# K and Q loaded at a unit's first step over two queues, row maxima 21 steps ahead, the first output weights loaded at the chunk's end

## The chip, the cores and the metric

The kernel runs on one core of one Trainium2 chip. The metric is the device time of one execution in microseconds (us), lower is better, as the median of several runs. Names used below: PE is the engine for matmuls, DVE the vector engine, ACT the scalar engine, POOL the GpSimd engine, SP the engine that only issues DMAs. The core has 16 DMA engines. DMAs are put to them through queues: q1 in the profile is filled by SP, q0 by POOL.

## The reference

One transformer block with conditioned layer norms, softmax attention with 32 heads of width 16, and a SwiGLU feed-forward part, for 2048 tokens of width 512, in float32:

```python
def _A_ref(x, wqkv, wo):
    B, S, D = x.shape
    H = 32; Dh = D // H
    qkv = (lambda x, *d: x.transpose(*d))((x @ wqkv).reshape(B, S, 3, H, Dh), 2, 0, 3, 1, 4)
    q, k, v = qkv[0], qkv[1], qkv[2]
    scale = Dh ** -0.5
    scores = jnp.einsum("bhqd,bhkd->bhqk", q, k) * scale
    p = _softmax(scores, axis=-1)
    o = jnp.einsum("bhqk,bhkd->bhqd", p, v)
    return (lambda x, *d: x.transpose(*d))(o, 0, 2, 1, 3).reshape(B, S, D) @ wo

def _B_ref(x, w_gate, w_up, w_down):
    g = _silu(x @ w_gate)
    u = x @ w_up
    return (g * u) @ w_down

mod = (_silu(c) @ w_mod).reshape(c.shape[0], 6, 1, -1)
sa, ca, ga, sb, cb, gb = (mod[:, 0], mod[:, 1], mod[:, 2], mod[:, 3], mod[:, 4], mod[:, 5])
h = _layernorm(x, axis=-1) * (1 + ca) + sa
x = x + ga * _A_ref(h, A_wqkv, A_wo)
h = _layernorm(x, axis=-1) * (1 + cb) + sb
x = x + gb * _B_ref(h, B_w_gate, B_w_up, B_w_down)
```

S is 2048, D is 512, F (the width of the feed-forward part) is 1792.

## The kernel before

**Stages.** The start (to about 190 us) computes Q, K and V. Each float32 operand is split in a high and a low half (`split`, L201), and a product is three matmuls (`mm3`, L205). Q and K are written to the DRAM tensors qd and kd, V stays on the chip in v_flat. The ten blocks of the weights wqs that are still to be split then are made by `weights` (L337): ACT writes the high half (L202) and the engine given to `split_w` the low half (L203), which is DVE for the blocks of K (j == 1) and POOL for the others. The bank of a projection is emptied by ACT (L367) and DVE (L369) into prt.

**Units and steps.** Attention runs over 32 units: unit u is a group of 4 heads (NG = 8 groups) and one of 4 chunks of 512 query tokens, with eight units to a chunk. A unit has 16 steps, one for each 128 keys. A step has four score matmuls (`score`, L506, each followed by an exp on ACT), four matmuls with their row maxima (`max_one`, L479 on PE and L481 on DVE) and the products with V (`pv_step`, L521). The maxima run `LEAD` = 20 steps ahead of the scores, so they belong to the next unit but one or the next. The first LEAD - 1 steps of maxima stand in a loop at the end of the start stage, between the last projection matmuls (`take(late, 9)`, nine matmuls to a step). When a unit's maxima are complete, `max_rows` (L483) reduces them on DVE, transposes them on PE (L491 to L493), and SP writes them as two further rows into the Q tile (L497, `qop<-mr`). The first score of that unit waits for this.

**Loads of a unit.** K of a unit goes into one of three kop tiles, Q into one of three qop tiles (`load_k`, `load_q`, `load_parts` at L401). The rows lie in two halves: partitions 0 to 47 and 64 to 111, one DMA for each half, 768 KB for K and 192 KB for Q. The function `before` puts the loads for unit u + 2 into the program ahead of step 6 of unit u. The tiles they write were last read by the scores of unit u - 1.

**The end of a unit** (`close_unit`, L836) comes two steps into the next: the denominators are copied out of the result o (`out_a`, `dn<-o`, L532), inverted on DVE (L536, two steps later), written to DRAM (L537, `d_dr<-dn`) and read back spread over all rows (L542, `rb<-d_dr`). All these DMAs are SP's. POOL multiplies (L548) and stores (L549). After the last unit of a chunk come the chunk's output weights wo (`load_wo`, L643): four steps after the close for chunk 0, one for the others.

**Filling.** From units 9, 17 and 25 on the steps of a chunk's successors are mixed with the output projection and the FFN of the finished chunk (`filled`, L944; the weights wgu and wd are loaded by SP, L652 and L657). A step without such work is called plain here, one with it filled. In units 1 to 7, POOL splits the FFN weights (`split_weights`, L575) and stores them to DRAM.

**What sets the order.** The kernel is written in the order of issue: each engine executes its instructions in the order of the program, and a wait of one holds everything behind it on the same engine. That holds for SP and POOL as issuers of DMAs too. An engine that has nothing to wait for runs ahead of the others.

Of the kernel before, what the change touches and what calls it, by code (L numbers as in the profile page):

```python
# [9 lines left out]
F32 = mybir.dt.float32  # L10
# [9 lines left out]
P = 128  # L20
S = 2048
D = 512
# [4 lines left out]
NK = D // P  # L27
NC = 4
CW = S // NC
NG = H // 4  # L30
NU = NG * NC
# [3 lines left out]
SCALE = DH ** -0.5  # L35
HD = D // 2
HQ = CW // 2
LEAD = 20
KR = 48
WIN = 3  # L40
HALVES = (2, 1, 1, 2)
# [1 line left out]
UG = 16 * NG  # L43
# [11 lines left out]
def run(it):  # L55
    for _ in it:
        pass


def take(it, k):  # L60
    run(islice(it, k))
# [40 lines left out]
def block_kernel(ctx, tc, x, wqkv, wo, w_gate, w_up, w_down, c, w_mod, out):  # L102
    nc = tc.nc
# [28 lines left out]
    qd = dram.tile([D, 3, S], F32, name="qd")  # L132
    kd = dram.tile([D, 3, S], F32, name="kd")
# [67 lines left out]
    def split(dst_h, dst_l, src, eng):  # L201
        nc.scalar.copy(dst_h, src)  # L202
        eng.tensor_sub(dst_l, src, dst_h.bitcast(F32))  # L203
# [11 lines left out]
    kop = [vp.tile([P, 2, S], F32R, name="kop0"), None, None]  # L215
# [20 lines left out]
    def stage(name):  # L236
        return pa.tile([P, NK, D], F32, name=name, tag="wst", bufs=3)
# [6 lines left out]
    def load_x(ci):  # L244
        xt[ci] = new_x()
        nc.sync.dma_start(xt[ci], xd[:, 4 * ci:4 * ci + 4, :])
# [6 lines left out]
    for ab in range(2):  # L253
        wm_ab.append(stage(f"wm_ab{ab}"))
        for e, v in enumerate((1, 0)):
            c0 = v * D + ab * HD
# [43 lines left out]
    def split_w(src, c0, eng=nc.gpsimd):  # L300
        cols = slice(c0, c0 + P)
        split(wqs[0][:, :, cols], wqs[1][:, :, cols], src, eng)
# [34 lines left out]
    def weights():  # L337
        st_ = {}
        for j, c0 in ((1, P), (0, P), (2, 0)):
            if j == 2:  # L340
                load_x(1)
            st_[j] = stage(f"wq_{j}")
            nc.sync.dma_start(st_[j][:, :, c0:D], wqd[:, :, j * D + c0:(j + 1) * D])
        yield
        for j, a in ((1, 1), (0, 1), (1, 2), (0, 2), (1, 3), (0, 3), (2, 0), (2, 1), (2, 2), (2, 3)):
            split_w(st_[j][:, :, a * P:(a + 1) * P], j * D + a * P, nc.vector if j == 1 else nc.gpsimd)
            yield

    def mods(va, vb, use):
# [10 lines left out]
    def proj_T(ci, w, m):  # L360
        def job():
            pt = bank("pt")
            col = (0 if w == 0 else D) + m * P

            def post():
                prt = pa0.tile([P, 2, CW], F32R, name="prt", tag="prt", bufs=4)
                nc.scalar.copy(prt[:, 0, :], pt)  # L367
                yield
                nc.vector.tensor_sub(prt[:, 1, :], pt, prt[:, 0, :].bitcast(F32))  # L369
                yield  # L370
                dst = (qd, kd)[w][m * P:(m + 1) * P, :, ci * CW:(ci + 1) * CW]
                nc.sync.dma_start(dst[:, 1 - w:3 - w, :], prt.bitcast(F32))
                nc.sync.dma_start(dst[:, 2 * w, :], prt[:, 0, :].bitcast(F32))
            return mm3(pt, lambda a, k: wqs[a][:, k, col:col + P], lambda b, k: hT[ci][b][:, k, :], NK), post()
        return job
# [12 lines left out]
    def proj_v(t):  # L388
        def job():
            pt = bank("pv_")  # L390
            sl = slice((t % 4) * P, (t % 4 + 1) * P)
            h_ = hT[t // 4]

            def post():
                nc.scalar.copy(v_sb[:, t, :, 0:DH], pt.rearrange("p (h d) -> p h d", d=DH))
                yield
            return mm3(pt, lambda a, k: h_[a][:, k, sl], lambda b, k: wqs[b][:, k, 2 * D:3 * D], NK), post()
        return job


    def load_parts(dst, src, g, c0, c1):  # L401
        heads = src[g * 64:(g + 1) * 64, :, c0:c1].rearrange("(s b d) r c -> b (d r) s c", s=2, b=2)
        for b in range(2):
            nc.sync.dma_start(dst[64 * b:64 * b + KR].bitcast(F32), heads[b])

    def load_k0(ci):
        load_parts(kop[0][:, :, ci * CW:(ci + 1) * CW], kd, 0, ci * CW, (ci + 1) * CW)
# [44 lines left out]
    qop, mx, pts, pv, o_, due, res = {}, {}, {}, {}, {}, {}, {}  # L452
# [7 lines left out]
            nc.sync.dma_start(kop[k][rows].bitcast(F32), kop[0][rows].bitcast(F32))  # L460

    def load_k(u):
        load_parts(kop[u % 3], kd, u % NG, 0, S)

    def load_q(u):
        ci, g = divmod(u, NG)
        qop[u] = pb.tile([P, 2, CW], F32R, name="qop", tag="qop", bufs=3)
        load_parts(qop[u], qd, g, ci * CW, (ci + 1) * CW)

    def max_one(r):  # L470

        u, t = divmod(r // 4, 16)
        b, e = 1 - r % 4 // 2, r % 2
        s, qt, kc = t // 8, t // 2 % 4, t % 2 * 2 + e
        if u not in mx:
            mx[u] = pb.tile([P, 2, 2, 4, NC], F32, name="mx", tag="mx", bufs=3)
        rows = slice(64 * b, 64 * b + KR)
        pm = four("pm")
        nc.tensor.matmul(pm, qop[u][rows, s, qt * P:(qt + 1) * P], kop[u % 3][rows, s, kc * CW:(kc + 1) * CW],  # L479
                         start=True, stop=True)  # L480
        nc.vector.tensor_reduce(mx[u][:, b, s, qt, kc:kc + 1], pm, op=ALU.max, axis=AX.X)  # L481
# [46 lines left out]
    def out_a(u, eng):  # L528
        pv.pop(u)
        o = o_.pop(u)  # L530
        dn = pf.tile([P, 16], F32, name="dn", tag="dn", bufs=1)
        eng.dma_start(dn, o[16:P:32, :].rearrange("h (b e) -> h b e", e=16))  # L532
        return o, dn

    def out_b(u, eng, o, dn):
        nc.vector.reciprocal(dn, dn)  # L536
        eng.dma_start(d_dr[u].rearrange("h (b e) -> (h b) e", e=16), dn)  # L537
        return o,

    def out_r(u, eng, o):  # L540
        rb = pf.tile([P, CW], F32, name="rb", tag="rb", bufs=1)
        eng.dma_start(rb, d_dr[u][:, None, :].to_broadcast([4, 32, CW]))  # L542
        return o, rb

    def out_c(u, eng, mul, o, rb):
        ci, g = divmod(u, NG)
        on = pf.tile([P, CW], F32, name="on", tag="on", bufs=1)
        mul.tensor_mul(on, o, rb)  # L548
        eng.dma_start(o_dr[ci, g], on)  # L549

    def at(i, f):
        due.setdefault(i, []).append(f)
# [7 lines left out]
    def tile_gu():  # L560
        return pf.tile([P, 4, NK, P], F32R, name="wgu", tag="wgu", bufs=2)
# [10 lines left out]
    def as_wo(w):  # L572
        return w.rearrange("p (b k) x c -> p b k (x c)", b=2)
# [53 lines left out]
    class Chunk:  # L627
# [12 lines left out]
        def load_x2(self, eng):  # L640
            eng.dma_start(self.x2, xd[:, 4 * self.ci:4 * self.ci + 4, :])

        def load_wo(self, places):  # L643
            self.wo = places
            for k, w in enumerate(places):
                (nc.sync if self.ci == 0 else nc.gpsimd).dma_start(w.bitcast(F32), wo_dr[k])

        def load_gu(self, f):
# [158 lines left out]
    chunks = {}  # L807
    side = []

    def begin(ci):  # L810
        x2 = pf.tile([P, 4, D], F32, name="x2", tag="x2", bufs=1)
        act = [pf.tile([P, NK, CW], F32R, name=f"act{a}", tag=f"act{a}", bufs=1) for a in range(2)]
        hT = [pf.tile([P, NK, CW], F32R, name=f"act{a}", tag=f"act{a}", bufs=1) for a in range(2)]
        chunks[ci] = ch = Chunk(ci, x2, act, hT)
        ch.load_x2(nc.gpsimd)
# [8 lines left out]
    def hook():  # L824
        while posts:
            posts.pop(0)()

    late = sm.jobs([proj_T(last, w, m) for w, m in kq[:1] + kq[2:]] + [proj_T(last - 1, w, m) for w, m in kq[6:]] +
                   [proj_T(last, *kq[1])] + [proj_v(4 * ci + t) for ci in (last - 1, last) for t in range(4)])
    ones_rows(1)  # L830
    load_q(0)
    take(late, 22)
    load_k0(last)
    take(late, 26)

    def close_unit(u, i):  # L836
        if u == NU - 1:
            res[u] = out_a(u, nc.scalar)
            return
        res[u] = out_a(u, nc.sync)  # L840
        at(i + 2, lambda: res.__setitem__(u, out_b(u, nc.sync, *res[u])))
        at(i + 3, lambda: res.__setitem__(u, out_r(u, nc.sync, *res[u])))
        at(i + 5, lambda: out_c(u, nc.gpsimd, nc.gpsimd, *res.pop(u)))
        if u % NG == NG - 1:
            if u // NG:
                at(i + 1, lambda: begin(u // NG))
            at(i + (1 if u // NG else 4), lambda: chunks[u // NG].load_wo([as_wo(tile_gu()) for _ in range(NK // 2)]))
            at(i + 7, lambda: chunks[u // NG].load_o(nc.gpsimd))
            at(i + 9, lambda: chunks[u // NG].split_o())

    at(3, lambda: begin(0))

    def before(i):

        u, kt = divmod(i + 1, 16)
        if kt == 6 and 1 <= u and u + 2 < NU:
            load_k(u + 2)
            load_q(u + 2)

# [2 lines left out]
    def after(i):  # L862
        nonlocal pf
        for f in due.pop(i, []):
            f()
        j = i + LEAD
        if j % 16 == 15 and j < n:
# [12 lines left out]

    for i in range(-LEAD, -1):
        if i == -LEAD + 3:
            load_k(1)
            load_q(1)
        for r in (0, 2, 1, 3):
            max_one(4 * (i + LEAD) + r)
        take(late, 9)
        after(i)
        while side:
            side.pop(0)()  # L890
# [5 lines left out]
    def pair_of():  # L896
        nonlocal done
        i = done // 4 - 1
        most = 4 * n - 4 * (LEAD - 1)
        if done % 4 == 0:  # L900
            before(i)
        score(i + 1, (ORDER if done < most else (0, 1, 2, 3))[done % 4])
        if done < most:
            max_one(done + 4 * (LEAD - 1))
        done += 1
# [157 lines left out]
```

## Time and profile before

| | us |
|---|---|
| median of 3 runs | 1898.84 (1897.57 to 1905.01) |
| the profiled execution | 1902.16 |
| its span, first to last instruction | 1900.4 |
| from the first score to the last | 189.0 to 1735.3 |

The span is that of the program's own instructions; the execution's time has 1.8 us around it. The profile's page has the busy time of each engine; views of the trace give the same for any stretch of the span, list who waited for whom, follow the chain of waits that ended last, and list the instructions of one engine in order of time. A DMA-issuing row of SP tells when SP issued a DMA, not when it landed. "PE bank L506 <- DMA qop<-mr" reads: the matmul of line 506 that writes a tile named bank waited for the DMA that writes qop from mr.

### The profile page before, as it was taken

The page shows a single profiled execution, that of the slowest core. Times are in us where ns is not written, and L with a number is a line of the kernel's source. Part 1 is how long each engine was busy: PE and PEld are TensorE (multiplying, and loading weights), DVE is VectorE, ACT ScalarE, POOL GpSimd, SP SyncE. Part 2 cuts the span into 40 slices and gives each one's busy share as a digit, 9 for nine tenths or more (in the row PEclk, how much of TensorE's full clock was granted, in tenths as well). Part 3 has the DMA queues.
Part 4 walks back from the last instruction along what each step waited for, and adds up shares of the span by engine and source line. Part 5 has one row for each costly group of instructions (what it writes and reads, how often), then busy time and mean ns, then how long its engine had stood idle before and what let it go on. Part 6 is the DMA issues. An engine that isn't in the chain of part 4 may idle for free.

```text
span 1900.4 us, 40767 instructions
## 1 busy us (share of the span) xinstructions
PE 1861.8 (98%) x16996; PEld 1147.7 (60%) x16996; DVE 1539.9 (81%) x2561; ACT 1249.2 (66%) x2330; POOL 381.8 (20%) x443
## 2 busy tenths in 40 slices
PE   6999999999999999999999999999999999999999
PEld 5776444444455666666555666666554466667787
DVE  5558999999999878888989888888999988841643
ACT  4221888888877766766777666766778876674211
POOL 3000544554122111111123111111123011121200
PEclk9999999999999999999999999999999999999999
DMA  8864767666362344543443345453543254243543
GB/s 283 279 224 120 222 166 184 177 190 195 88 147 71 112 120 121 160 108 96 135 102 72 116 114 155 121 142 75 142 89 68 55 143 121 101 158 132 233 189 111
DMA packets 79732, 267.60 MB, mean 141 GB/s; under 512 B 17364, under 2 KB 22484, under 8 KB 58868
## 3 DMA queue, kind: packets, MB, share of 16 engines
q1 hardware_dynamic: 64684, 202.32, 39.4%
q0 software_dynamic: 14176, 61.88, 9.4%
q8 instruction: 133, 2.18, 0.5%
q10 hardware_dynamic: 688, 0.80, 0.1%
q14 instruction: 51, 0.42, 0.1%
HBM read 201.85 MB, written 62.13 MB: 139 GB/s over the span
## 4 chain that ended last, share of the span: by engine, by line
PE 88%; DMA 6%; DVE 3%; ACT 2%; SPq 1%; issue 0%; ACTq 0%; DVEq 0%
PE bank L521 25%; PE bank L506 21%; PE bank L718 18%; PE bank L479 9%; PE bank L727 6%; PE bank L209 6%; DMA wgu<-gu_dr 3%; DVE mx L481 1%; DMA qop<-qd 1%; DMA qop<-mr 1%; DVE stt L743 1%; PE bank L491 1%; PE bank L162 0%; DMA wm_ab<-in_w_mod 0%; PE bank L703 0%
## 5 line engine op out<-in xcount | busy, mean ns | idle before, releaser
L481 DVE TENSOR_REDUCE mx<-bank 128x1 f32<-128x512 f32 x2048 | 1282.4, 682 | 149.3 <-PE bank L479 90.7
L479 PE MATMUL bank<-kop,qop 48*128 48x512 f32 x2048 | 757.4, 433 | 4.2 <-DVE mx L481 2.1
L506 PE MATMUL bank<-qop,kop 50*128 50x512 f32 x2048 | 745.6, 428 | 8.3 <-DMA qop<-mr 5.5
L506 PEld LDWEIGHTS bank<-qop,kop 50*128 50x128 f32 x2048 | 343.6, 185 | 316.7 <-issue 53.4
L479 PEld LDWEIGHTS bank<-kop,qop 48*128 48x128 f32 x2048 | 341.5, 185 | 30.4 <-DVE mx L481 10.3
L718 PE MATMUL bank<-act,wgu 64*128 64x512 f32 x1872 | 300.7, 396 | 4.9 <-DMA wgu<-gu_dr 4.7
L718 PEld LDWEIGHTS bank<-act,wgu 64*128 64x128 f32 x1872 | 187.5, 188 | 38.1 <-issue 4.7
L548 POOL TENSOR_TENSOR on<-o,rb 128x512 f32<-128x512 f32 x31 | 39.8, 1285 | 519.9 <-DMA rb<-d_dr 423.9
L718 PE MATMUL bank<-wd,mid 64*128 64x512 f32 x912 | 130.4, 392 | 0.0
L779 POOL CAST mid<-m 128x512 fp32r<-128x512 f32 x40 | 24.5, 613 | 449.1 <-PE bank L506 261.5
L209 PE MATMUL bank<-hT,wqs 128*128 128x512 f32 x384 | 97.1, 404 | 3.9 <-DVE prt L369 2.4
L718 PEld LDWEIGHTS bank<-wd,mid 64*128 64x128 f32 x912 | 88.6, 186 | 15.2 <-issue 0.7
L209 PEld LDWEIGHTS bank<-hT,wqs 128*128 128x128 f32 x384 | 71.6, 191 | 26.2 <-issue 5.9
L775 DVE SCALAR_TENSOR_TENSOR q<-th,bank 128x512 f32<-128x512 f32 x56 | 38.1, 681 | 54.3 <-ACT th L771 54.3
L771 ACT ACTIVATE th<-bank 128x512 f32<-128x512 f32 x56 | 33.2, 593 | 58.7 <-PE bank L727 58.4
L791 DVE TENSOR_TENSOR x<-bank,x 128x512 f32<-128x512 f32 x84 | 53.9, 685 | 19.3 <-PE bank L718 19.3
L369 DVE TENSOR_TENSOR prt<-bank,prt 128x512 fp32r<-128x512 f32 x32 | 21.9, 688 | 47.4 <-ACT prt L367 47.4
L367 ACT CAST prt<-bank 128x512 fp32r<-128x512 f32 x32 | 18.8, 587 | 60.2 <-PE bank L209 46.8
L777 DVE TENSOR_TENSOR m<-bank,q 128x512 f32<-128x512 f32 x56 | 38.7, 691 | 21.1 <-PE bank L727 19.1
L727 PE MATMUL bank<-wd,mid 128*128 128x512 f32 x216 | 52.3, 394 | 0.5 <-DVE mid L780 0.3
L780 POOL TENSOR_TENSOR mid<-m,mid 128x512 fp32r<-128x512 f32 x40 | 51.4, 1286 | 3.3
L718 PE MATMUL bank<-wgu,act 64*128 64x512 f32 x288 | 47.9, 395 | 0.0
(6281 smaller groups left out, 5111.1 us busy)
## 6 DMA issues: line engine op xcount, KB each, us to landing
wgu<-gu_dr SPq DMA_DIRECT2D x48, 1024.0 KB
kop<-kd SPq DMA_DIRECT2D x62, 768.0 KB
wd<-wd_dr SPq DMA_DIRECT2D x28, 1024.0 KB
gu_dr<-wgu POOLq DMA_DIRECT2D x14, 1024.0 KB, 4.1
qop<-qd SPq DMA_DIRECT2D x64, 192.0 KB
kd<-prt SPq DMA_DIRECT2D x16, 512.0 KB
qd<-prt SPq DMA_DIRECT2D x16, 512.0 KB
kop<-gu_dr SPq DMA_DIRECT2D x8, 1024.0 KB
```

Source lines behind the costliest of these rows:

```text
L209: nc.tensor.matmul(pt, lhs(a, k), rhs(b, k), start=(n == 0), stop=(n == 3 * nk - 1))
L479: nc.tensor.matmul(pm, qop[u][rows, s, qt * P:(qt + 1) * P], kop[u % 3][rows, s, kc * CW:(kc + 1) * CW], start=True, stop=True)
L481: nc.vector.tensor_reduce(mx[u][:, b, s, qt, kc:kc + 1], pm, op=ALU.max, axis=AX.X)
L506: nc.tensor.matmul(sp, kop[u % 3][rows, h // 2, kt * P:(kt + 1) * P], qop[u][rows, h // 2, :], start=True, stop=True)
L521: nc.tensor.matmul(pv[u][32 * h:32 * h + 32, cols], v_flat[:, e0:e0 + 32], p_[h][:, cols], start=(kt == 0 and half == 0), stop=(kt == 15), ...
L548: mul.tensor_mul(on, o, rb)
L718: nc.tensor.matmul(outs[e], lhs(e, a, k)[rows], rhs(b, k)[rows], start=(ph == 0 and j == 0), stop=(ph == 1 and j == z))
L727: nc.tensor.matmul(outs[e], lhs(e, a, k), rhs(b, k), start=(j == 0), stop=(j == z))
L775: nc.vector.scalar_tensor_tensor(q, th, 1.0, outs[0], op0=ALU.add, op1=ALU.mult)
L777: nc.vector.tensor_mul(m32, outs[1], q)
L780: (nc.gpsimd if slow else nc.vector).tensor_sub(mid[:, 1, :], m32, mid[:, 0, :].bitcast(F32))
L791: nc.vector.tensor_add(ch.x2[:, t, :], outs[e], ch.x2[:, t, :])
```

## The change

There are five edits. K and Q of unit u + 2 are asked for ahead of step 1 of unit u instead of step 6, and from unit 3 on the second half of the rows is issued by POOL instead of SP. LEAD is 21 instead of 20, so that one more step of maxima stands in the start; the projection matmuls between them are taken as nine and eight in turn. The low halves of the K blocks of wqs are made by POOL instead of DVE. The output weights of chunk 0 are loaded in the last step but one of its last unit (step UG - 2 = 126 of all) instead of four steps after that unit's close. For the other chunks the load stays where it was.

```diff
-LEAD = 20
+LEAD = 21
...
-            split_w(st_[j][:, :, a * P:(a + 1) * P], j * D + a * P, nc.vector if j == 1 else nc.gpsimd)
+            split_w(st_[j][:, :, a * P:(a + 1) * P], j * D + a * P)
...
-    def load_parts(dst, src, g, c0, c1):
+    def load_parts(dst, src, g, c0, c1, second=nc.sync):
         heads = src[g * 64:(g + 1) * 64, :, c0:c1].rearrange("(s b d) r c -> b (d r) s c", s=2, b=2)
         for b in range(2):
-            nc.sync.dma_start(dst[64 * b:64 * b + KR].bitcast(F32), heads[b])
+            (second if b else nc.sync).dma_start(dst[64 * b:64 * b + KR].bitcast(F32), heads[b])
...
     def load_k(u):
-        load_parts(kop[u % 3], kd, u % NG, 0, S)
+        load_parts(kop[u % 3], kd, u % NG, 0, S, nc.gpsimd if u > 2 else nc.sync)
...
-        load_parts(qop[u], qd, g, ci * CW, (ci + 1) * CW)
+        load_parts(qop[u], qd, g, ci * CW, (ci + 1) * CW, nc.gpsimd if u > 2 else nc.sync)
...
-        def load_wo(self, places):
-            self.wo = places
-            for k, w in enumerate(places):
+        def load_wo(self, places=None):
+            self.wo = places or [as_wo(tile_gu()) for _ in range(NK // 2)]
+            for k, w in enumerate(self.wo):
...
             if u // NG:
                 at(i + 1, lambda: begin(u // NG))
-            at(i + (1 if u // NG else 4), lambda: chunks[u // NG].load_wo([as_wo(tile_gu()) for _ in range(NK // 2)]))
+                at(i + 1, lambda: chunks[u // NG].load_wo())
...
     at(3, lambda: begin(0))
+    at(UG - 2, lambda: chunks[0].load_wo())
...
-        if kt == 6 and 1 <= u and u + 2 < NU:
+        if kt == 1 and 1 <= u and u + 2 < NU:
             load_k(u + 2)
             load_q(u + 2)
...
-        take(late, 9)
+        take(late, 9 if i % 2 else 8)
```

What stands on SP's queue in a plain unit (the first of them), before the change. A row has the line, the operation, out<-in, the shape, and x2 where two alike follow each other; kop tiles carry their numbers:

```order
L497 DMA qop<-mr 2x8x128 x2
L532 DMA dn<-o 128x1x16
L537 DMA d_dr<-dn 128x16
L542 DMA rb<-d_dr 128x1x512
L404 DMA kop_87<-kd 48x2x2048 x2
L404 DMA qop<-qd 48x2x512 x2
```

And at the same place after it:

```order
L497 DMA qop<-mr 2x8x128 x2
L404 DMA kop_87<-kd 48x2x2048
L404 DMA qop<-qd 48x2x512
L532 DMA dn<-o 128x1x16
L537 DMA d_dr<-dn 128x16
L542 DMA rb<-d_dr 128x1x512
```

One half of K and one of Q stand ahead of the denominators; the other halves are now on POOL. The next place is SP's queue in a unit that is filled with FFN work (unit 11), before the change:

```order
L532 DMA dn<-o 128x1x16
L537 DMA d_dr<-dn 128x16
L542 DMA rb<-d_dr 128x1x512
L404 DMA kop_961<-kd 48x2x2048 x2
L404 DMA qop<-qd 48x2x512 x2
L657 DMA wd<-wd_dr 128x2048
L652 DMA wgu<-gu_dr 128x2048 x2
```

After it:

```order
L532 DMA dn<-o 128x1x16
L404 DMA kop_961<-kd 48x2x2048
L404 DMA qop<-qd 48x2x512
L537 DMA d_dr<-dn 128x16
L542 DMA rb<-d_dr 128x1x512
L657 DMA wd<-wd_dr 128x2048
L652 DMA wgu<-gu_dr 128x2048 x2
```

Here dn stays ahead of K, and K and Q move ahead of the two steps that wait for DVE and for the DMA d_dr; the FFN weights wd and wgu stay behind them all. The last place is DVE in the start stage, as one piece of the difference:

```order
 L331 TENSOR_TENSOR hT_136<-h_232,hT_135 128x512
 L331 TENSOR_TENSOR hT_136<-h_234,hT_135 128x512
-L203 TENSOR_TENSOR wqs_115<-wq_198,wqs_114 128x4x128 x3
 L369 TENSOR_TENSOR prt<-bank_68,prt 128x512
 L369 TENSOR_TENSOR prt<-bank_69,prt 128x512
```

The three subtractions that stood ahead of the first two prt are gone from DVE; they now alternate with the three that POOL had already.

## Prediction

> **What bounds the kernel now.** I read the page first, then the busy time of each engine by stretches of the span, then who waits for whom on PE, and last the DMA issues of SP in order of time. The page says only that PE is busy nearly throughout:
>
> ```profile
> PE 1861.8 (98%) x16996; PEld 1147.7 (60%) x16996; DVE 1539.9 (81%) x2561; ACT 1249.2 (66%) x2330; POOL 381.8 (20%) x443
> ```
>
> That hides two kinds of stage. I cut the span at the first score matmul (L506; 64 in a unit) of each unit. A row gives length, busy us and instructions of PE, weight load, DVE, ACT and POOL, then the granted clock, the DMA share and GB/s.
>
> ```profile
> 467.20:505.90 38.70, 38.64 (x392) 18.18 (x392) 38.60 (x66) 33.64 (x68) 10.14 (x9) 1.00 0.51 148
> 348.10:388.80 40.70, 40.34 (x390) 18.49 (x390) 38.12 (x65) 33.57 (x66) 19.48 (x21) 0.96 0.66 183
> 189.00:547.30 358.30, 352.17 (x3487) 163.99 (x3487) 349.61 (x595) 306.48 (x603) 157.08 (x154) 1.00 0.65 176
> 928.30:970.50 42.20, 41.15 (x402) 18.77 (x398) 39.38 (x67) 34.60 (x69) 12.04 (x15) 0.96 0.61 161
> 708.30:764.00 55.70, 55.70 (x572) 36.77 (x570) 48.08 (x78) 38.23 (x69) 5.68 (x6) 1.00 0.46 119
> 1127.70:1183.50 55.80, 55.80 (x574) 36.62 (x572) 48.17 (x78) 38.29 (x69) 5.68 (x6) 1.00 0.46 119
> 647.30:708.30 61.00, 58.56 (x600) 39.07 (x596) 48.70 (x77) 39.28 (x71) 7.54 (x8) 0.97 0.37 95
> 1239.40:1299.90 60.50, 58.45 (x600) 38.59 (x598) 48.78 (x77) 39.32 (x71) 7.53 (x8) 0.97 0.38 95
> 820.00:877.30 57.30, 57.06 (x600) 37.67 (x596) 48.64 (x77) 39.28 (x71) 7.55 (x8) 1.00 0.41 101
> 1071.00:1127.70 56.70, 56.70 (x598) 37.23 (x594) 48.63 (x77) 39.25 (x71) 7.56 (x8) 1.00 0.40 101
> ```
>
> A plain unit (no output or FFN work mixed in) is bound by DVE: undisturbed, unit 7 takes 38.7 us with DVE busy 38.60, so a step is 2.42 us. A unit filled with FFN matmuls is bound by PE: units 12 and 20 take 55.7 and 55.8 us. Against these floors the other rows have excess: units 0 to 8 take 358.3 where 9 x 38.7 is 348.3 (10.0 over), unit 16 has 3.5, and units 11, 22, 14 and 19 have 5.2, 4.7, 1.5 and 0.9 over 55.8, together 12.3. What ends last in those places is on PE's list of waits (total, times, longest) and in the chain of waits:
>
> ```profile
> PE bank L506 <- DMA qop<-mr: 5.5, 4, 1.8
> PE bank L718 <- DMA wgu<-gu_dr: 4.7, 3, 2.4
> PE bank L209 <- DVE prt L369: 2.4, 1, 2.4
> PE bank L479 <- DMA qop<-qd: 1.0, 1, 1.0
> 541.74 5.45 DMA qop<-mr
> 671.70 17.31 DMA wgu<-gu_dr
> 944.88 16.32 DMA qop<-qd
> 690.00:693.50 3.50, 3.50 (x20) 3.27 (x18) 1.80 (x3) 1.69 (x3) 0.00 (x0) 0.51 0.04 12
> ```
>
> Few microseconds of PE idle, but they cost more than they last: after unit 11's wait of 2.4 us the clock was granted at 0.51 for 3.4 us (last row), and in a plain unit DVE has to be refilled.
>
> **The change, part by part.** *K and Q earlier.* Today SP takes them up late, because it is held by the denominators (dn, d_dr, rb) of the unit before. These are unit 6, then unit 11:
>
> ```profile
> 428.48 0.50 PE L506 MATMUL bank<-qop,kop 50*128 50x512 f32 x1
> 432.94 0.59 SPq L532 DMA_DIRECT2D dn<-o  x1
> 440.14 0.24 DVE L536 RECIPROCAL dn<-dn 128x16 f32<-128x16 f32 x1
> 441.89 0.55 SPq L542 DMA_DIRECT2D rb<-d_dr  x1
> 442.53 0.90 SPq L404 DMA_DIRECT2D kop<-kd  x2
> 665.99 0.90 SPq L404 DMA_DIRECT2D kop<-kd  x2
> 671.32 0.34 SPq L657 DMA_DIRECT2D wd<-wd_dr  x1
> 671.70 12.62 SPq L652 DMA_DIRECT2D wgu<-gu_dr  x2
> 943.42 0.90 SPq L404 DMA_DIRECT2D kop<-kd  x2
> ```
>
> K goes out 14.05 us into unit 6, though written for its step 6. Moved to step 1 it stands on SP ahead of dn and waits only for the last score of the unit before, so I expect it at about the unit's first score: 14 us sooner. In unit 16 K and Q, issued at 943.42, kept PE waiting until 961.2, 17.8 us later; with 14 us in hand (11.6 when LEAD takes its step) that wait goes: I count **3.0** of unit 16's 3.5. In unit 11 the FFN weights wgu stand behind K, Q and wd and end at 689.0, 23 us after K's issue. With K started at step 1 (3.5 us a step) and the weights still at step 7, some 20 us lie between them, more than 17.8, so this collision goes; unit 22 is the same place 11 units on, 14 and 19 weaker cases. Weight loads at other steps meet K anew: in units 12 and 20 wd and wgu are due two steps (7 us) after K; what is left of K by then (up to 10.8 us) and 2 MB at the 413 GB/s below (5 us) is 15.8 against the 14 us until they are used: 0 to 2 us each, and I take 0. I count **12** for the FFN units.
>
> *LEAD 21.* The row maxima of a unit are finished one step sooner, so mr goes out 2.4 us sooner. Its four waits are at most 1.8 us, so they go. *First output weights earlier.* The last and worst of them, before unit 9, stood behind 2 MB:
>
> ```profile
> 522.01 0.92 SPq L646 DMA_DIRECT2D wgu<-wo_dr  x2
> 541.15 1.13 SPq L497 DMA_DIRECT2D qop<-mr  x2
> 135.00:189.00 54.00, 53.24 (x237) 35.00 (x236) 46.57 (x77) 8.11 (x15) 0.00 (x0) 1.00 0.57 158
> 1578.30:1634.30 56.00, 56.00 (x586) 37.48 (x584) 48.08 (x77) 39.04 (x71) 7.58 (x8) 1.00 0.50 143
> 1689.90:1735.30 45.40, 45.40 (x492) 30.18 (x492) 8.07 (x13) 34.29 (x65) 12.88 (x15) 1.00 0.39 126
> ```
>
> wo was 19 us ahead of mr there, so what delayed mr is less sure than the others (weight traffic of POOL is near too); LEAD covers its 1.8 us either way, and the move by itself I cost at nothing. Of the 10.0 us in units 0 to 8 I count **9**. LEAD also moves one step of four maxima (PE pairs and 4 x 0.6 us of DVE) from the filled end to the start. At the end a step with maxima costs 56.0/16 = 3.50 and one without 45.4/16 = 2.84: 0.66 us saved. In the start stage PE is nearly full (53.24 of 54), the projection matmuls are only spread thinner (8 or 9 a step), and DVE has 7.4 us free: 0.66 us lost if PE-bound, 2.4 if DVE-bound. Net 0 to +1.8; I take **+0.5**.
>
> *Low halves of three weight blocks from DVE to POOL.* At the start PE waits 2.40 us for the first prt, which stands on DVE behind them:
>
> ```profile
> 23.98 3.19 DVE L203 TENSOR_TENSOR wqs<-wq,wqs 128x512 fp32r<-128x512 f32 x2 [0.18 <-ACT wqs L202]
> 27.10 1.28 DVE L369 TENSOR_TENSOR prt<-bank,prt 128x512 fp32r<-128x512 f32 x2
> 27.83 0.79 PE L209 MATMUL bank<-hT,wqs 128*128 128x512 f32 x1 [2.40 <-DVE prt L369]
> 1456.00:1470.50 14.50, 1.00 0.86 173
> 684.00:688.00 4.00, 2.71 (x38) 1.24 (x36) 3.63 (x6) 2.40 (x5) 1.40 (x2) 1.00 1.00 413
> ```
>
> Without them prt starts when ACT has made its half, some 1.5 us sooner; then POOL's chain of six blocks is next, at about 1.3 us each against 3 us of matmuls per block, so it keeps ahead. **1.5**, between 0 and 2.4.
>
> *Two queues.* SP issues two DMAs a unit fewer and POOL two more. These cost POOL under 1 us each beside 10 to 20 us of work per 38.7 (rows above): hidden. Behind POOL's new wait stand the weight splits, which now cannot run ahead of the unit; they have the whole unit. What is not hidden is **dn**: it now stands on SP's queue behind half of K and Q, and DVE, the bound, executes the reciprocal in order. From 428.48 to 440.14 there are 11.7 us. K and Q are 1.97 MB (2 x 768 KB and 2 x 192 KB). At unit 26's rate, 173 GB/s over K's stretch, they take 11.4 us before dn's own landing; at the 413 GB/s that wgu gets, 4.8. So dn's lateness is between nothing and, by the 17.8 us of unit 16, some 6 us a unit. The two halves write different partitions (0 to 47 and 64 to 111) and are now in flight together instead of one behind the other. I take the fast end, that they do run side by side: **0**.
>
> 173 fits the Trainium skill's SBUF — State Buffer, section "Door 1: The DMA port swizzle", by which partitions 0..63 reach 8 of 16 ports (218 GB/s) and 64..127 the other 8. But its section "Can I just issue two DMAs to hit both halves?" says No, a pair measured +6%, and that other issuing engines don't help; by it the first rival below happens (1921). The rows above cannot tell, since before the change the halves never start together.
>
> Sum on the profiled span: -3 - 12 - 9 + 0.5 - 1.5 = -25; I take 1 us back for meetings of K with weights, and get -24: 1900.4 to 1876. That execution took 1902.16 in all, 3.3 above the median 1898.84; the same gain on the median gives **1875**.
>
> **Rivals.** *The halves serialize and DVE waits for dn.* By the order K stands ahead of dn in 17 units (1 to 10, 16 to 18, 24 to 27). With 11.4 us, 1 us to start and 2 for dn itself it lands 14.4 us into the unit, 2.7 late: 17 x 2.7 = 46 lost, 22 net: 1921. It decides from a lateness of 24/17 = 1.4 us, where the change is worth nothing. For it: DMA share 0.86 in K's stretch, engines nearly full. Against: that share is of engines held by slow packets at 173 of 413 GB/s. *Some of it:* dn 0.3 to 1 us late, or a weight load of units 12, 20, 28 late again with its slow clock: 5 to 17 of the 24 are given back, 1880 to 1892. *The change does nothing:* SP takes K up no earlier because something else holds it, or POOL's half comes late enough to be waited for; then only LEAD and the start gain, 5 to 10 less: 1889 to 1896. Against: SP is idle from mr to dn in every plain unit.
>
> **How the numbers follow.** Forecast 0.52 (1868 to 1880); some given back 0.22; serialized 0.17 (1900 to 1935); nothing 0.09. A measurement of this kernel tells 0.5%, 9.5 us, from no change, so the line is 1889.3. Faster: 0.52 and most of the second, 0.69; same: the rest of it, the last and the mild end of serialized, 0.17; slower 0.14. The range 1867 to 1902 leaves out most of the serialized case.
>
> **What would show it.** Right: K's issues at each plain unit's first score; no PE wait on qop<-mr, qop<-qd or wgu; plain units near 38.7 and units 11 and 22 near 55.8; no granted clock of 0.5 after the start. Wrong: idle time of DVE before L536 put down to DMA dn<-o, plain units above 40 throughout, or a stretch of K and Q still at 173 to 190 GB/s.

## The result, and the profile after the change

The changed kernel takes 2018.37 us (median of six runs, 2011.00 to 2026.96) where the kernel before takes 1902.12 (six runs, 1897.57 to 1905.01): a ratio of 1.0616, 95% interval 1.058 to 1.0652. It is slower by 6%, outside the predicted range. The profiled executions have spans of 1900.4 us before and 2020.8 after.

First the page after: busy time, the chain of work that ended last, and one group of instructions (busy, mean ns, idle before it and its releaser).

```profile
PE 1898.7 (94%) x16996; PEld 1156.0 (57%) x16996; DVE 1539.9 (76%) x2558; ACT 1252.0 (62%) x2330; POOL 419.6 (21%) x504
PE 81%; DMA 12%; DVE 3%; ACT 3%; issue 0%; SPq 0%; ACTq 0%; DVEq 0%
L536 DVE RECIPROCAL dn<-dn 128x16 f32<-128x16 f32 x32 | 8.0, 248 | 113.7 <-DMA dn<-o 113.7
```

DVE's busy time is that of before to the digit; its idle time is new. 32 reciprocals that work for 8.0 us are waited for 113.7 us, and DMA stands in the chain with 12% (6% before). The lists of waits say the same from both sides (total, times, longest):

```profile
DVE dn L536 <- DMA dn<-o: 113.7, 18, 11.3
PE bank L479 <- DVE mx L481: 97.5, 23, 10.8
```

Before the change the same two waits were these:

```profile
DVE dn L536 <- DMA dn<-o: 7.3, 1, 7.3
PE bank L479 <- DVE mx L481: 2.1, 7, 0.3
```

PE waits for the maxima (mx), because DVE, which makes them, stands at the reciprocal. One of the 18 waits is old: in every kernel here the reciprocal after the last unit waits 6 to 8 us for its dn (7.3 before, 6.5 in the changed kernel). The other 17 lie in units 1 to 10, 16 to 18 and 24 to 27. What happens in unit 1, first SP's queue, then DVE, in order of time (start, duration):

```profile
226.71 0.31 SPq L404 DMA_DIRECT2D kop<-kd  x1
228.18 0.31 SPq L404 DMA_DIRECT2D qop<-qd  x1
232.27 0.62 SPq L532 DMA_DIRECT2D dn<-o  x1
249.15 0.34 SPq L537 DMA_DIRECT2D d_dr<-dn  x1
248.87 0.25 DVE L536 RECIPROCAL dn<-dn 128x16 f32<-128x16 f32 x1 [9.37 <-DMA dn<-o]
```

K and Q go out at the unit's first score, as meant. But dn, issued at 232.27, lands only when the reciprocal starts, 16.6 us later, and DVE has run out of other work 9.37 us before. Three stretches of time show what that costs (length, busy us of PE, weight load, DVE, ACT and POOL, granted clock, DMA share, GB/s): unit 1 of the kernel before, unit 1 of the changed kernel, and a part of the latter.

```profile
227.40:267.90 40.50, 38.85 (x394) 18.13 (x392) 39.93 (x68) 34.68 (x69) 18.97 (x19) 1.00 0.63 177
228.00:279.20 51.20, 42.38 (x394) 19.52 (x390) 39.04 (x68) 33.75 (x68) 20.44 (x21) 0.87 0.52 143
244.10:257.80 13.70, 8.08 (x47) 3.62 (x51) 7.12 (x13) 3.66 (x7) 2.07 (x3) 0.50 0.33 133
```

The same work takes 10.7 us more: the wait and, from before its end on, TensorE at a granted clock of 0.50 for 13.7 us. In the attention stage the trace has 17 such half-clock stretches, 143 us in all; before there were four, 13.7 us in all.

What was forecast to go did go. PE's list has no wait for wgu, qd or mr any more, and units 11 and 22, which took 61.0 and 60.4 us, take 56.7 each. The losses are in the plain units. The last column is the best version found below, in which K and Q are asked for directly behind dn; units are cut at their first score, in us:

| stretch | before | changed | K directly behind dn |
|---|---|---|---|
| start to first score | 189.0 | 188.5 | 187.1 |
| units 0 to 8 | 358.3 | 437.7 | 350.5 |
| units 9, 10 | 100.0 | 107.1 | 100.2 |
| unit 11 | 61.0 | 56.7 | 56.7 |
| unit 12 | 55.8 | 55.8 | 57.2 |
| units 13 to 15 | 164.3 | 163.9 | 163.8 |
| units 16 to 18 | 142.7 | 161.3 | 139.5 |
| units 19 to 23 | 280.7 | 276.7 | 277.1 |
| units 24 to 27 | 170.8 | 196.7 | 171.1 |
| units 28 to 31 | 212.9 | 212.8 | 213.0 |
| after the last score | 165.1 | 163.8 | 165.8 |
| span | 1900.4 | 2020.8 | 1882.1 |

### The profile page after: what moved, and what is told of

Read it like the earlier page. It is cut to its first block, busy times and chain, and to the rows that moved or that the text cites. A ratio compares the mean times of both kernels' runs of the same rounds, so it can differ in the third digit from the quotient of the medians.

```text
span 2020.8 us, 40832 instructions
## 1 busy us (share of the span) xinstructions
PE 1898.7 (94%) x16996; PEld 1156.0 (57%) x16996; DVE 1539.9 (76%) x2558; ACT 1252.0 (62%) x2330; POOL 419.6 (21%) x504
## 4 chain that ended last, share of the span: by engine, by line
PE 81%; DMA 12%; DVE 3%; ACT 3%; issue 0%; SPq 0%; ACTq 0%; DVEq 0%
PE bank L521 23%; PE bank L506 18%; PE bank L718 17%; DMA dn<-o 11%; PE bank L479 9%; PE bank L727 6%; PE bank L209 6%; DVE mx L481 1%; PE bank L491 1%; ACT o L525 0%; DVE stt L743 0%; PE bank L162 0%; DMA wm_ab<-in_w_mod 0%; PE bank L493 0%; PE bank L492 0%
## 5 line engine op out<-in xcount | busy, mean ns | idle before, releaser
L479 PE MATMUL bank<-kop,qop 48*128 48x512 f32 x2048 | 774.0, 444 | 99.4 <-DVE mx L481 97.5
L506 PE MATMUL bank<-qop,kop 50*128 50x512 f32 x2048 | 764.4, 437 | 3.0 <-ACT v_flat L395 0.2
L506 PEld LDWEIGHTS bank<-qop,kop 50*128 50x128 f32 x2048 | 352.3, 189 | 319.1 <-issue 63.4
L479 PEld LDWEIGHTS bank<-kop,qop 48*128 48x128 f32 x2048 | 351.0, 189 | 136.1 <-DVE mx L481 120.8
L718 PE MATMUL bank<-act,wgu 64*128 64x512 f32 x1872 | 296.1, 392 | 0.0
L718 PEld LDWEIGHTS bank<-wd,mid 64*128 64x128 f32 x912 | 88.6, 186 | 15.2 <-issue 0.7
L536 DVE RECIPROCAL dn<-dn 128x16 f32<-128x16 f32 x32 | 8.0, 248 | 113.7 <-DMA dn<-o 113.7
L404 POOL DMA_DIRECT2D kop<-kd x29 | 17.0, 587 | 233.4 <-PE bank L506 116.9
L777 DVE TENSOR_TENSOR m<-bank,q 128x512 f32<-128x512 f32 x56 | 38.7, 691 | 21.1 <-PE bank L727 19.1
## 6 DMA issues: line engine op xcount, KB each, us to landing
kop<-kd POOLq DMA_DIRECT2D x29, 768.0 KB, 12.2
gu_dr<-wgu POOLq DMA_DIRECT2D x14, 1024.0 KB, 10.2
```

Source lines behind the costliest of these rows:

```text
L506: nc.tensor.matmul(sp, kop[u % 3][rows, h // 2, kt * P:(kt + 1) * P], qop[u][rows, h // 2, :], start=True, stop=True)
L718: nc.tensor.matmul(outs[e], lhs(e, a, k)[rows], rhs(b, k)[rows], start=(ph == 0 and j == 0), stop=(ph == 1 and j == z))
L777: nc.vector.tensor_mul(m32, outs[1], q)
```

## The experiments

**Why is dn late?** Three theories stood at the start: its place on SP's queue behind half of K and Q; the traffic of K and Q wherever it stands; or another part of the change. Four kernels, each one change away from the changed one. *K at step 3*, on the same two queues, so that dn goes out ahead of it:

```diff
-        if kt == 1 and 1 <= u and u + 2 < NU:
+        if kt == 3 and 1 <= u and u + 2 < NU:
```

> The changed kernel with K and Q asked for at a unit's step 3 instead of step 1, on the same two queues: dn now stands ahead of them on SP, all else stays. Order theory (dn waits because it stands behind half of K and Q on SP's queue): dn lands 2 to 5 us after its issue in plain units, the reciprocals' waits (113.7 us in the changed kernel) fall below 5 us, units 1 to 6 go back from 50 to 53 us to 39 to 41, time 1874 to 1890. Traffic theory (any K in flight on either queue slows dn's 128 small packets, wherever it stands): dn still lands 6 to 15 us after its issue, waits of 50 us or more, 1930 to 2010. Other-part theory (the maxima a step earlier, the weight splits or the output weights cost the time): no change, 2005 to 2030.

*All on SP*, still at step 1 (the same edit in load_q):

```diff
-        load_parts(kop[u % 3], kd, u % NG, 0, S, nc.gpsimd if u > 2 else nc.sync)
+        load_parts(kop[u % 3], kd, u % NG, 0, S)
```

> The changed kernel with all of K and Q on SP's queue, still at step 1: dn stands behind 1.97 MB instead of 0.98 MB there, and nothing of K and Q is on POOL's queue. Order theory: dn lands later than in the changed kernel or as late, 11 us of K and Q plus some 2 us of its own after step 1, so the reciprocals wait for 110 to 250 us in all: 2010 to 2120. Traffic theory (POOL's half beside SP's is what slows dn): dn lands sooner, waits of 50 us or less, 1900 to 1960. Other-part theory: 2005 to 2030.

*All on POOL*, still at step 1 (`load_k` and `load_q` name POOL from u = 3 on, and no engine before):

```diff
-            (second if b else nc.sync).dma_start(dst[64 * b:64 * b + KR].bitcast(F32), heads[b])
+            (second or nc.sync).dma_start(dst[64 * b:64 * b + KR].bitcast(F32), heads[b])
```

> The changed kernel with all of K and Q on POOL's queue, still at step 1: dn has SP's queue to itself, while the same 1.97 MB is in flight beside it. Order theory: dn lands 2 to 5 us after its issue, reciprocals' waits below 10 us, plain units 39 to 42, 1874 to 1895. Traffic theory: dn lands 6 to 15 us after its issue as in the changed kernel, 1960 to 2040. Other-part theory: 2005 to 2030.

*Reciprocal three steps later*, loads as in the change; what follows the reciprocal (rb, the product, the chunk's loads and splits of o) moves by three steps too:

```diff
-        at(i + 2, lambda: res.__setitem__(u, out_b(u, nc.sync, *res[u])))
+        at(i + 5, lambda: res.__setitem__(u, out_b(u, nc.sync, *res[u])))
...
-        at(i + 5, lambda: out_c(u, nc.gpsimd, nc.gpsimd, *res.pop(u)))
+        at(i + 8, lambda: out_c(u, nc.gpsimd, nc.gpsimd, *res.pop(u)))
```

> The changed kernel with the reciprocal and all that follows it (stores of d_dr, rb, the product, the chunk's output loads) three steps later, so that DVE has some 7.3 us more until it executes the reciprocal; the loads stay as in the changed kernel. Order theory and traffic theory alike (DVE's in-order wait for dn is the loss): dn lands as late as before, the 113.7 us of waits shrink to what is over 7.3 us each (8 waits of 8 to 11 us leave 5 to 30 us), the half-clock stretches go with them, 1880 to 1925. Other-part theory: 2005 to 2030.

They took 1930.24, 1990.34, 2033.23 and 1916.20 us (one run each; the kernel before took 1903.75 on that chip). DVE's wait for dn in each, in this order:

```profile
DVE dn L536 <- DMA dn<-o: 44.6, 9, 12.6
```

```profile
DVE dn L536 <- DMA dn<-o: 81.6, 18, 10.9
```

```profile
DVE dn L536 <- DMA dn<-o: 128.5, 26, 11.6
```

```profile
DVE dn L536 <- DMA dn<-o: 27.6, 8, 7.0
```

The order theory falls as the whole cause. With SP's queue to itself (third run) dn lands 17.0 us after its issue in unit 1, as late as in the change; and issued ahead of K on SP (first run) it still takes 5 to 11 us in units 1 to 9 and 18 in units 16 and 24, with POOL's half beside it. All on SP, where the order theory expected the most, is faster than the change itself. There dn still lands 8 to 13 us after its issue in units 1 to 9, so K ahead of it on its own queue makes it late too; the time lies in none of the three expected ranges. The first and the third run lie in the traffic theory's ranges by time (in the first the waits are 44.6 us, where 50 or more were expected). The other-part theory falls with the last run: the loads as in the change, only more time until dn is needed, and 102 of the 116 us of loss over before are gone. The half-clock stretches did not all go with them: seven are left, 37 us.

How traffic alone does it is seen in the DMA of the all-on-POOL kernel, in two stretches after dn's issue at 231.70 (packets, MB, share of the 16 engines): until 240.4, and from there until it landed.

```profile
DMA packets 278, 1.33 MB, mean 153 GB/s; under 512 B 60, under 2 KB 60, under 8 KB 171
q0 software_dynamic: 278, 1.33, 101.7%
...
DMA packets 693, 3.08 MB, mean 359 GB/s; under 512 B 198, under 2 KB 198, under 8 KB 439
q0 software_dynamic: 559, 3.05, 91.6%
q1 hardware_dynamic: 132, 0.01, 1.2%
```

POOL's queue is q0, SP's is q1. For 8.7 us the 16 engines are full of q0's packets, and not one of dn's 128 packets starts. Then they come, but strung out over 7.5 us between the larger packets of POOL's weight traffic. In the kernel before, the engines had room when dn was issued (231.2 to 235.0), and it landed 1.9 us after its issue:

```profile
q0 software_dynamic: 67, 0.42, 26.4%
q1 hardware_dynamic: 132, 0.01, 1.9%
```

The Trainium skill's DMA: Bandwidth & Descriptors, section "Queues, rings and completion order", has each DMA engine go round between the queues packet by packet, draining "a whole packet" of several descriptors from one before it switches. That agrees in kind with the first part, where K's packets are drained for 8.7 us before one of dn's. That dn's packets are then taken a few at a time over 7.5 us does not follow from it.

**What is the rest worth, and is it the place or the second queue?** Three kernels. *K at step 3, all on SP*: both edits of the first two runs.

> The changed kernel with K and Q at step 3 and all on SP's queue: dn is ahead of them there and POOL's queue carries none of them; the maxima a step earlier, the weight splits and the output weights stay as in the change. Meeting theory (dn's small packets are late when K's packets are in flight, ahead of them on SP's queue or beside them on POOL's; both have to go): dn lands 2 to 5 us after its issue, the reciprocals' waits are below 10 us, plain units at 39 to 41, no new half-clock stretches, 1872 to 1888. Rival (K's packets overtake dn even from behind it on one queue): waits of 30 us or more, 1905 to 1940.

*The rest alone*: K at step 6, on SP, as before the change (kt == 6, and the edit of the second run).

> K and Q as before the change (step 6, SP's queue); what is left of the change is the maxima 21 steps ahead, the weight splits on one engine and the output weights earlier. Meeting theory: no waits for dn at all; by the prediction's terms (9 + 1.5 gained, 0.5 lost) 10 us faster than before, 1889 to 1897. Other-part theory (these parts cost some of the time lost): 1905 or more.

*Two queues at step 6*: of the change only the step is undone (kt == 6).

> The change with only the step undone: K and Q are over two queues, at step 6, behind dn, d_dr and rb. Meeting theory: dn is through before K is asked for, so its waits are below 10 us and the time is that of the kernel with neither (1885 to 1898); two queues by themselves cost nothing and, as both ways of loading took 13 to 15 us for K in the runs so far, win nothing. Two-queue theory (POOL's K requests and their wait hold up its weight work and the rest): 1905 or more.

Measured, beside 1900.81 us for 19 runs of the kernel before: K at step 3 on SP 1903.74 us (10 runs), ratio 1.0013 (0.9998 to 1.0029); the rest alone 1905.52 (10 runs), ratio 1.0039 (1.0016 to 1.0062); two queues at step 6 1921.14 (one run). The waits for dn behaved as expected in the first, 8.1 us with the old one in it. But neither of the two won anything, and the third lost: by time the meeting theory misses all three. The first lies between its two ranges, the second at the edge of the other-part theory's (4.7 us over before, not the 116 of the change), the third in the two-queue theory's, though for another reason. In the third, POOL's queue explains it (POOL, then SP, by time):

```profile
226.48 0.60 POOL L404 DMA_DIRECT2D kop<-kd  x1 [5.63 <-PE bank L479]
230.31 0.61 SPq L532 DMA_DIRECT2D dn<-o  x1
237.81 0.34 SPq L537 DMA_DIRECT2D d_dr<-dn  x1
243.86 0.43 SPq L404 DMA_DIRECT2D kop<-kd  x1
```

SP's half stands behind dn, d_dr and rb and goes out at 243.86. POOL's half is written at the same step but waits only for its buffer, and POOL has no denominators ahead of it: it goes out 17.4 us sooner and meets dn (9 waits, 29.4 us). So at step 6 the second queue brings 22 us of waits for dn that the rest alone (7.6 us) does not have. Its 15.6 us over the rest alone are less sure: one run, where that kernel's ten reach 1920.94.

In the rest alone (first row: PE) the maxima one step earlier meet a Q that is not earlier; in the kernel with K at step 3 (PE throughout, then POOL in unit 15) rb stands behind K on SP, POOL waits for it, and the FFN's mid behind it comes late:

```profile
PE bank L479 <- DMA qop<-qd: 8.5, 9, 1.5
```

```profile
PE bank L718 <- POOL mid L779: 7.3, 4, 2.6
POOL on L548 <- DMA rb<-d_dr: 33.8, 1, 33.8
```

Units 12, 15 and 23 grew by 4.9, 5.0 and 6.7 us over before there, more than its other units had won.

**K directly behind dn, and fewer packets.** The first kernel asks for K and Q where dn is issued, on SP (the request in `before` is left out, and POOL is not named in `load_k` and `load_q`):

```diff
         res[u] = out_a(u, nc.sync)
+        if u + 3 < NU:
+            load_k(u + 3)
+            load_q(u + 3)
```

> K and Q all on SP's queue and asked for directly behind dn, in every unit (step 1 or 2 of it); the rest of the change stays. At step 3 (the run before) dn was on time but units 12, 15 and 23 grew by 4.9, 5.0 and 6.7 us over before and POOL's mid was waited for. Theory (rb, now behind K on SP, held POOL's product and, in order behind it, POOL's FFN work; asked for some 5 to 7 us sooner K is through in time): units 12, 15 and 23 within 1.5 us of 55.8, 51.4 and 51.7, units 1 to 8 at 38.7 to 40.7, dn's waits below 12 us, 1884 to 1893. Rival (rb behind K holds POOL wherever K is asked for): 1898 to 1906.

The other two lay dn over fewer partitions, in the all-on-POOL kernel and in the changed one:

```diff
-        dn = pf.tile([P, 16], F32, name="dn", tag="dn", bufs=1)
-        eng.dma_start(dn, o[16:P:32, :].rearrange("h (b e) -> h b e", e=16))
+        dn = pf.tile([32, 64], F32, name="dn", tag="dn", bufs=1)
+        eng.dma_start(dn, o[16:P:32, :].rearrange("h (b e) -> h b e", e=64))
```

> The kernel with all of K and Q on POOL's queue at step 1 (2033 us; dn 16 to 17 us after its issue in units 1 to 6), with dn laid over 32 partitions of 64 sums instead of 128 of 16: the same 8 KB in 32 packets of 256 bytes instead of 128 of 64, two instead of eight for each DMA engine; reciprocal and d_dr follow. Turn theory (each small packet waits its turn behind packets of the other queue): dn lands 3 to 7 us after its issue, its waits fall from 128.5 to below 40 us, 1890 to 1940. Rival (dn waits for what is already in the engines or for a free way into memory, whatever the number of its packets): dn still lands 10 us or more after its issue, 2000 to 2035.

> The changed kernel, again with dn in 32 packets of 256 bytes instead of 128 of 64; K and Q stay on two queues at step 1. Turn theory: what is left is the half of K and Q ahead of dn on SP (it lands 7 to 12 us after the unit's start) and two turns beside POOL's half: dn lands 4 to 9 us after its issue, waits of 10 to 60 us, 1890 to 1960. Rival (the number of packets does not matter): 2005 to 2030.

K directly behind dn is faster than both kernels: 1885.24 us (five runs, 1882.23 to 1895.97) beside 1901.10 before (eight runs), ratio 0.993 (0.9899 to 0.9961), a gain of 0.7%. All signs expected of its theory came. Its busy times, its wait for dn and unit 1:

```profile
PE 1856.1 (99%) x16996; PEld 1145.2 (61%) x16996; DVE 1536.7 (82%) x2558; ACT 1249.8 (66%) x2330; POOL 385.5 (20%) x446
```

```profile
DVE dn L536 <- DMA dn<-o: 6.3, 1, 6.3
```

```profile
225.50:264.40 38.90, 38.90 (x392) 18.30 (x390) 38.63 (x67) 33.58 (x67) 13.59 (x14) 1.00 0.62 153
```

Unit 1 stands at DVE's floor with the clock at 1.00; dn lands 1.9 to 5.4 us after its issue in all units, and DVE's only wait for it is the old one, 6.3 us. Units 12, 15 and 23 take 57.2, 51.4 and 51.7: rb is still behind K, but POOL's wait for it in unit 15 is 29.7 us instead of 33.8, and PE waits for no mid of POOL any more.

Fewer packets brought 2008.83 us (from 2033.23) and 1992.12 (from 2018.37), one run each. The waits of the all-on-POOL version, and its DMA from dn's issue at 232.2 for 8.8 us and from there to the landing:

```profile
DVE dn L536 <- DMA dn<-o: 89.1, 28, 6.3
```

```profile
q0 software_dynamic: 272, 1.32, 100.8%
q1 hardware_dynamic: 1, 0.00, 0.0%
...
q0 software_dynamic: 277, 1.04, 98.9%
q1 hardware_dynamic: 35, 0.01, 1.8%
```

The first part stays, 8.8 us with one packet of q1; the second shrinks to 3.4 us. dn lands 10.6 to 12.0 us after its issue in units 1 to 8, where with 128 packets it took 16 to 17 in units 1 to 6. So both theories hold for a part each: turns explain some 5 us, and the larger 9 us are K's packets that dn finds in the engines. By the times the turn theory alone is missed in both (below 1940 and 1960); the first lies in its rival's range, the second below its rival's. 9 us are enough to stop DVE, and units 9 and 10 became some 3 us longer each than with 128 packets, which stayed unexplained.

**Does the gain need both, K early and the maxima early?** *The kernel before, with K directly behind dn and nothing else:*

> The kernel before with one edit: K and Q asked for directly behind dn on SP's queue instead of at step 6; maxima 20 steps ahead, weight splits and output weights as before. If the gain of the last version (1882 profiled, 18 under before) came from K and Q alone: 1882 to 1888. If the maxima's extra step carries its part of units 0 to 8 (waits for mr, 5.5 us in before, and what follows on them): units 11, 16 and 22 gain as there (4, 3 and 4 us) and units 0 to 8 keep 3 to 8 us of their excess over 350.5: 1886 to 1893. If neither (the gain needs both): 1895 or more.

*The best version with the maxima 20 steps ahead* (LEAD = 20, nine jobs at each step of the start):

> The version with K and Q directly behind dn, weight splits and output weights as in the change, but maxima 20 steps ahead as before. Against the run beside it, it tells what the splits and the output weights give (by the prediction 1.5 and 0 us: 1 to 2 us less); against the version with 21 it tells the extra step: PE's waits for mr come back (5 us or so) and the time is 3 to 8 us over that version's 1885, 1887 to 1892; if the extra step is worth nothing once K is early, 1883 to 1887.

The first took 1912.03 us (1897.99 to 1925.39), ratio 1.0051 (1.0014 to 1.0087); the second 1908.69, ratio 1.0038 (0.9994 to 1.0082). The first came out as the last of its three cases, that the gain needs both; the second is slower than either of its cases. Units 11 and 22 gain there too (56.8 each), but units 0 to 8 take 362.1 and 366.3 us in their profiles. The profiled executions took 1898.41 and 1903.67 us, less than the medians (of the first kernel's ten runs four lie near 1898 and six between 1911 and 1925), so no trace shows what the slower runs lose. In the second, unit 2's first score shows one loss (PE's wait, then the stretch from there):

```profile
PE bank L506 <- DMA qop<-mr: 2.5, 1, 2.5
```

```profile
269.40:283.10 13.70, 12.85 (x78) 5.29 (x82) 7.14 (x12) 6.73 (x13) 5.36 (x7) 0.50 0.71 233
```

mr, issued at 264.65, took 5.3 us to land; the score waited 2.5 us; and the clock was granted at 0.50 for 13.7 us. Unit 2, which begins when that wait ends, takes 45.4 us there and 39.3 in the best version, where mr took 1.7 us and landed 2.3 us before the score: 6.1 us more behind a wait of 2.5. mr is the same kind of transfer as dn, a few small packets. What it meets here is not K, which had landed 15 us before, but POOL's weight traffic: while mr was in flight POOL's queue moved 1.55 MB and SP's 0.02. POOL's weight store is issued 1.1 us ahead of mr here (263.54) and 0.7 us behind it in the best version (260.48, after 259.78).

## Why the prediction was wrong, step by step

- **The step that failed** is the one on dn under *Two queues*: "I take the fast end, that they do run side by side: 0". dn was 6.3 us late on average, in the 17 units that the order had named, 107 us in all (113.7 less the old wait, 6.5 there). Its bound of "some 6 us a unit" was near; I chose the wrong end. That it was near is in part luck: it supposed K ahead of dn on SP, and the waits, 2.7 to 11.3 us, come as well with nothing ahead of dn there (all on POOL). The halves side by side win nothing: from K's first issue to the landing of its second half the changed kernel takes 15.2 us (median of 30 units), all on SP at step 1 13.4, before 15.2. The Trainium skill's section that the prediction set against this (SBUF — State Buffer, "Can I just issue two DMAs to hit both halves?") says No; these times agree.
- **The mechanism** was not the one I priced either. The first rival let dn queue behind K on SP: 2.7 us late, 46 us. Two things made it more: dn's first packet starts only when the packets that K and Q have put on the engines are nearly through, on whichever queue (in the 17 units of the changed kernel 6.3 to 9.4 us after dn's issue, and at most 1.7 us before POOL's half of K and Q has landed); and POOL's further traffic then strings it out.
- **"These cost POOL under 1 us each … hidden"** counted POOL's time and not where its traffic falls. POOL waits at its K request until the unit before is done (12.2 us at 228.44 in the changed kernel), its weight loads and stores bunch behind it, and between dn's issue and landing POOL's queue moves 4.1 MB in unit 1; in units 17 and 25 it moves 1 MB and dn takes some 10 us instead of 17.
- **The clock** had no term. The changed kernel's span is 138.7 us over that of the best version; 107 are waits for dn (113.7 less 6.3), some 31 are left over. That these go with the half-clock stretches is seen in unit 1 and in the last experiment's unit 2; no run separates them from DVE's refilling.
- **K and Q earlier, 3 + 12**: right in kind. In the best version unit 16 goes from 42.1 to 39.3 (2.8), units 11, 14, 19 and 22 give 4.3, 0.6, 0.1 and 3.8, together 8.7. The 12 was too large because I gave all of them the floor of units 12 and 20; units with about 600 matmuls keep PE busy for 56.7 us:

```profile
637.80:694.50 56.70, 56.70 (x598) 37.18 (x594) 48.57 (x77) 39.41 (x71) 7.59 (x8) 1.00 0.43 102
```

- **K meeting the FFN weights in units 12 and 20, 0 to 2 each**: 1.5 and 0.4 in the best version, none in the change; the 1 us taken back covers it.
- **LEAD and the output weights, 9**: 7.8 in the best version (358.3 to 350.5; even there the floor of 9 x 38.7 is not reached), but as part of a pair. Without early K and Q the earlier maxima wait for Q (ratio 1.0039); without the earlier maxima, early K leaves PE's waits for mr at 6.2 us (5.5 before), and the time is no better (1.0038). The sum added them as if each stood by itself.
- **The start, 0.5 lost and 1.5 gained**: start and end together take 354.1 before, 352.2 in the change and 352.9 in the best version, and PE's wait for the first prt fell from 2.4 to 0.8 us. Right in kind and near in size.

Without the dn term the sum of -24 was near: the best version's profiled span is 18.2 us under before, its median 15.9, though it asks for K behind dn and on one queue.

## What to carry to other kernels

A transfer of a few KB on which an in-order engine waits has a deadline; in these runs a bulk load that started just ahead of it, on either queue, made it miss that deadline, so order the small transfer first and give the bulk load the time behind it. Before moving a load earlier, list the small transfers that its new place meets, and read from the trace whether the engines had room when these were issued: 1.9 us where they had room says nothing of a busy stretch. And edits that give each other room (data earlier, its use earlier) can each be worth less than nothing alone.

## What the runs showed of the hardware beyond what I expected

- A second queue gave a small transfer no way past a load in flight: in unit 1 of the all-on-POOL kernel 8.7 us with no packet of dn's, and 17 us to land 8 KB.
- A request on POOL's queue is not held by the step it is written at: with the same code position SP's half went out 17.4 us after POOL's.
- After one wait of 2.5 us TensorE's clock stayed at 0.50 for 13.7 us, though PE was busy for 12.85 of them; after one of 2.4 us in unit 11 of the kernel before it was 3.4. What decides between them stayed open. Every half-clock stretch in the attention stage of all these traces lasted 3.4, 6.8, 10.2 or 13.7 us.
- Versions near the edge scatter: ten runs of the kernel with K directly behind dn alone lie between 1898 and 1925 us, fourteen of the kernel before beside it between 1891 and 1906.
